# Top-32 attention and two MLPs on one core: the first search step read half from PSUM, head by head

## The chip, the cores and the metric

The kernel runs on one NeuronCore of one Trainium2 chip. The metric is device time in microseconds (us) from one launch. A profiled execution gives a trace with the start and duration of each instruction; its span runs from the first to the last instruction. The engines are TensorE (PE, matmuls into PSUM; PEld is its weight load), VectorE (DVE), ScalarE (ACT), GpSimd (POOL) and SyncE (SP, which only issues transfers here). Each executes its own instructions in a fixed order and waits on semaphores of the others.

## The reference

Attention over 4 batches, 8 heads, 576 positions of width 64, in which each row keeps only its 32 largest scores, then two MLPs on the 2304 resulting rows:

```python
scores = scale * np.matmul(q, k.transpose(0, 1, 3, 2))          # (4, 8, 576, 576)
kth = np.partition(scores, -32, axis=-1)[..., -32:-31]
scores = np.where(scores >= kth, scores, -1e9)
attn = softmax(scores)                                          # rows sum to 1
x = heads_merged(attn @ v)                                      # (2304, 512)
h = x @ w_in                                                    # 512 -> 2048
x = (P(h) / Q(|h|, h*h)) @ w_out                                # P cubic, Q quadratic
h = x @ w2_in
out = (h * np.cos(h)) @ w2_out
```

All in float32.

## The kernel before

Attention is cut into 72 units. A unit is one tile of 128 query rows with one pair of heads: `qk(i)` makes the scores of both heads (`j` is 0 or 1), `topk(i)` finds the 32nd largest of each row, `av(i)` transposes the weights on TensorE and multiplies them with the values. The MLPs follow some units behind in steps `(k, g)`: `in1`, `copy1`, `pol1`, `rec1`, `mid1`, `end1`, `low1`, `out1` for the first (their tiles are `w`, `q`, `r`, `u`, `gg`), `in2` to `out2` for the second.

In `qk`, TensorE writes the scores of one head into `sx`, a PSUM tile of two banks: columns 0 to 287 in one half, 288 to 575 in the other. ScalarE copies them to SBUF, into `sS` (three buffers). There is one `sx`, so the second head's matmuls wait until the first head's copy has been read from it. The spare columns of `sx` serve `av`.

In `topk`, VectorE first takes the larger and the smaller of each score in the left half and its partner in the right half, into the tile `e` (two buffers): two instructions over both heads, 576 columns each. From the larger ones MAX (the eight largest of each row, into `hd`) and MATCH_REPLACE (strike these out) make the first sixteen, then both work over all 576 columns. ScalarE writes the exponentials into `e`, and a SCALAR_TENSOR_TENSOR masks and sums them. A new `e` needs an older one to have been transposed by `av`.

Beside this run 64 conversions (`conv`) of the weights, given in float64, into a high and a low float32 part: SP loads a piece into `raw` (a ring of five buffers, three for the later 32), ScalarE makes two numbers of it, VectorE shifts one (`cb`, a TENSOR_SCALAR), GpSimd adds the two, and the parts are split and stored. GpSimd also does `u` and `q` products, some low parts, and the split of `k` (`store_k`, which follows `qk` in units 1, 3, 5 and 7 and writes `kdr`).

In units 0 to 19 (`U0` is 20) a list scheduler decides the order on each engine, from the order of the code, the data dependencies and a window on how far an engine may run ahead. From unit 20 to 71 the order on the engines is that of the code in `unit`. `free` writes the units before 20: its generator makes `qk(i + 1)`, then steps `topk(i)` and `av(i - 1)` in five pieces, between which `early` puts the MLP steps.

Of the kernel before, what the change touches and what calls it, by code (L numbers as in the profile page):

```python
# [10 lines left out]
F32 = mybir.dt.float32  # L11
# [4 lines left out]
ALU = mybir.AluOpType  # L16
# [3 lines left out]
B, H, S, D = 4, 8, 576, 64  # L20
# [3 lines left out]
P = 128  # L24
# [4 lines left out]
HALF = S // 2  # L29
# [30 lines left out]
OBB, EB, SB = 1, 2, 3  # L60
QRB, QB = 2, 2
S0 = 46
U0, U1 = 20, 72
# [56 lines left out]
def body(tc, out, qt, kt, vt, ident_d, w1_d, w1o_d, a_d, b_d, w2_d, w2o_d):  # L120
    nc = tc.nc
    V, A = InOrder(tc, nc.vector, WIN, C0), InOrder(tc, nc.scalar, WA, PA)
# [3 lines left out]
    with ExitStack() as ctx:  # L126
        def pool(name, bufs=1, **k):
            return ctx.enter_context(tc.tile_pool(name=name, bufs=bufs, **k))
# [4 lines left out]
        att = pool("att", 2)  # L133
# [25 lines left out]
        sx = ps_s.tile([P, 2, 512], F32, name="sx")  # L159
# [17 lines left out]
        def store_k(*a):  # L177
            for _ in split_k(*a):
                pass

        def prep(b, pr):
            x = kv.tile([P, 2, S], F32R, tag="k", bufs=KB, name=f"kraw{b}_{pr}")
            SP.dma_start(out=x[:, 0].bitcast(F32), in_=kt[b, pr])
            return x
# [126 lines left out]
        st, et, sums = {}, {}, {}  # L311
# [3 lines left out]
        def halves(ap):  # L315
            return ap.rearrange("p (a c) -> p a c", a=2)

        def after(mm, bank):
            for x in order[bank]:
                tc.add_manual_dep(mm.ins, x, mybir.DependencyInfo(mybir.DependencyClass.NoSync, mybir.DependencyReason.DATA), reason="bank")  # L320

        def qk(i):
            n, pr = units[i]
            raw, x = qs_.pop(i)
            hi, lo = (x[:, 0], x[:, 1]) if x is not None else (None, None)
            kvs = ins[i]
            m = P // len(kvs)
            st[i] = sb = att.tile([P, 2, S], F32, tag="sS", bufs=SB, name=f"sS{i}")
            for j in range(2):
                rows = slice(j * D, (j + 1) * D)  # L330
                for c, (k, _) in reversed(list(enumerate(kvs))):
                    qs = slice(0, (c + 1) * m)
                    for hf in range(2):
                        o = sx[qs, hf, :HALF]
                        hs = slice(hf * HALF, (hf + 1) * HALF)
                        if n < 2:
                            mm = PE.matmul(o, raw[rows, j, qs], k[rows, 0, hs].bitcast(F32), start=True, stop=True)
                            after(mm, hf)
                        elif i < QH:
                            mm = PE.matmul(o, raw[:, j, qs], k[:, j, hs].bitcast(F32), start=True, stop=True)  # L340
                            after(mm, hf)
                        else:
                            mm = PE.matmul(o, hi[:, j, qs], k[:, j, hs], start=True, stop=False, skip_group_check=True)
                            after(mm, hf)
                            mm = PE.matmul(o, lo[:, j, qs], k[:, j, hs], start=False, stop=True, skip_group_check=True)
                        order[hf] = [mm.ins.name]
                A.activation(halves(sb[:, j]), sx[:, :, :HALF], AF.Copy)
                if j == 0:
                    yield
            if n == 1:  # L350
                store_k(kvs[0][0], 0, pr)

        def topk(i):
            n, pr = units[i]
            sc = st.pop(i)
            tiles = [sc[:, j] for j in range(2)]
            e = att.tile([P, 2, S], F32, tag="e", bufs=EB, name=f"e{i}")
            et[i] = e
            kb, t = n // 2, n % 2
            if i % 8 == 0:  # L360
                sums[kb] = sml.tile([P, 2, H], F32, tag="sum", bufs=2, name=f"sum{kb}")
            sm = sums[kb][:, t]
            hds = sml.tile([P, 2, 32], F32, tag="hd", bufs=2, name=f"hd_{i}")
            hd = [hds[:, j] for j in range(2)]
            nb = sml.tile([P, 2], F32, tag="nb", bufs=2, name=f"nb_{i}")
            big = [e[:, j, :HALF] for j in range(2)]
            both = [e[:, j] for j in range(2)]

            def top(j, x, r):
                V.max(out=hd[j][:, 8 * r:8 * r + 8], in_=x[j])  # L370

            def drop(j, x, r):
                V.match_replace(out=x[j], in_to_replace=hd[j][:, 8 * r:8 * r + 8], in_values=x[j], imm_value=NEG)

            l, r = sc[:, :, :HALF], sc[:, :, HALF:]
            grouped = U0 <= i < U1
            V.tensor_tensor(e[:, :, :HALF], l, r, op=ALU.max)
            if not grouped:
                top(0, big, 0)
                yield  # L380
            V.tensor_tensor(e[:, :, HALF:], l, r, op=ALU.min)
            if not grouped:
                top(1, big, 0)
            yield
            first = ((top, big, 0), (drop, big, 0), (top, big, 1))
            for step in (first[0 if grouped else 1:], ((drop, big, 1), (top, both, 2)), ((drop, both, 2),)):
                for f, *x in step:
                    for j in range(2):
                        f(j, *x)
                yield  # L390
            for j, s in enumerate(tiles):
                top(j, both, 3)
                if j == 0:
                    A.activation(nb, hds[:, :, 0], AF.Copy, scale=-SCALE)
                A.activation(e[:, j], s, AF.Exp, bias=nb[:, j:j + 1], scale=SCALE)
            yield
            for j, s in enumerate(tiles):
                row = sm[:, 2 * pr + j:2 * pr + j + 1]
                V.scalar_tensor_tensor(e[:, j], s, hd[j][:, 31:32], e[:, j], op0=ALU.is_ge, op1=ALU.mult, accum_out=row)
                yield  # L400
# [369 lines left out]
        def free(i, prev):  # L770
            nq = qk(i + 1) if i + 1 < nu else iter(())
            next(nq, None)
            next(nq, None)
            if i + 2 < nu:
                load_k(i + 2)
            t = topk(i) if i < nu else iter([None] * 9)
            fresh = []
            for p in range(5):
                if p == 0:
                    for x, a in held:  # L780
                        store_k(x, *a)
                    held[:] = [(prep(*a), a) for a in preps.get(i, [])]
                    if prev is not None:
                        next(prev)
                    next(t, None)
                    if prev is not None:
                        next(prev)
                    next(t, None)
                    if prev is not None:
                        a = av(i - 1)  # L790
                        next(a)
                        next(a, None)
                        if i % 4 == 0:
                            nrm.append(norm((i - 1) // 8, (i - 1) // 4 % 2))
                            next(nrm[-1])
                            next(nrm[-1])
                            fresh.append(nrm[-1])
                    if 0 < i < nu:
                        load_v(i)
                else:  # L800
                    next(t, None)
                if p == 1 and i < U0:
                    load_q(i + 3)
                if fresh and p == 1:
                    next(fresh.pop())
                if len(nrm) == 2 and p in (1, 4):
                    for x in nrm[:1] if p == 1 else nrm[1:]:
                        next(x)
                        next(x, None)
                    if p == 4:  # L810
                        nrm.clear()
                if i == U0 - 1 and p == 4:
                    for _ in qk(i + 2):
                        pass
                    load_k(i + 3)
                    high_q(i + 3)
                    load_q(i + 4)
                yield t
# [54 lines left out]
        def unit(i, prev):  # L873
            sine = (i - UB - 1) % SINB == SINB - 1
            t = topk(i)
            if i > U0:
                V.ahead = G.last
# [82 lines left out]

        load_k(1)
        load_v(0)
        for _ in qk(0):
            pass
        load_q(2)
        prev = None
        for u in range(UB + NB * NG + 3):
            grouped = U0 <= u < U1
            f = free(u, prev) if not grouped and u <= nu else iter(())
# [55 lines left out]
```

## Time and profile before

| | us |
|---|---|
| median of three runs (1339.94 to 1340.45) | 1340.32 |
| the profiled execution, its own time | 1339.15 |
| its span | 1337.4 |
| TensorE busy in the span | 1233.8 |
| VectorE busy | 1156.0 |
| ScalarE busy | 1093.7 |
| GpSimd busy | 569.6 |

Units 0 to 19 fill the first quarter of the span; in it all engines share the work of attention, of the conversions and, from unit 9, of the first MLP. An engine's busy share over the whole span mixes this part with the later ones, so it has to be read stage by stage. In rows of the trace all instructions stand under one line, L80, where a helper records them; they are told apart by their tiles.

### The profile page before, as it was taken

The page shows a single profiled execution, that of the slowest core. Times are in us where ns is not written, and L with a number is a line of the kernel's source. Part 1 is how long each engine was busy: PE and PEld are TensorE (multiplying, and loading weights), DVE is VectorE, ACT ScalarE, POOL GpSimd, SP SyncE. Part 2 cuts the span into 40 slices and gives each one's busy share as a digit, 9 for nine tenths or more (in the row PEclk, how much of TensorE's full clock was granted, in tenths as well). Part 3 has the DMA queues.
Part 4 walks back from the last instruction along what each step waited for, and adds up shares of the span by engine and source line. Part 5 has one row for each costly group of instructions (what it writes and reads, how often), then busy time and mean ns, then how long its engine had stood idle before and what let it go on. Part 6 is the DMA issues. An engine that isn't in the chain of part 4 may idle for free.

```text
span 1337.4 us, 25132 instructions
## 1 busy us (share of the span) xinstructions
PE 1233.8 (92%) x8992; PEld 1086.7 (81%) x8992; DVE 1156.0 (86%) x2498; ACT 1093.7 (82%) x1871; POOL 569.6 (43%) x469
## 2 busy tenths in 40 slices
PE   6675678888999999999999999999999999999998
PEld 3343455656889999999989899999999999999996
DVE  6999879979799999999999999999999998755633
ACT  7887788886888898888898888888898888877753
POOL 2656444453245555445554444454444444430000
PEclk9676999999999999999999999999999999999999
DMA  8986777884356777667677776666677778877774
GB/s 254 335 278 223 247 239 246 275 311 132 122 190 217 231 245 248 215 218 229 208 234 239 246 230 210 213 217 200 217 234 265 268 283 288 297 235 235 235 258 155
DMA packets 155948, 314.98 MB, mean 236 GB/s; under 512 B 12592, under 2 KB 47536, under 8 KB 155824
## 3 DMA queue, kind: packets, MB, share of 16 engines
q1 hardware_dynamic: 122832, 261.99, 59.3%
q10 hardware_dynamic: 32992, 51.39, 12.0%
q8 instruction: 71, 1.16, 0.4%
q14 instruction: 53, 0.43, 0.1%
HBM read 278.20 MB, written 35.13 MB: 234 GB/s over the span
## 4 chain that ended last, share of the span: by engine, by line
PE 62%; DVE 13%; ACT 12%; DMA 4%; issue 4%; POOL 3%; ACTq 1%; SPq 0%; POOLq 0%; DVEq 0%
PE h L80 24%; PE o L80 12%; PE sx L80 10%; PE y L80 10%; DVE e L80 6%; DVE hd L80 3%; ACT r L80 2%; DVE u L80 2%; DMA raw<-w 1%; ACT sS L80 1%; ACT e L80 1%; ACT cb L80 1%; PE diff L80 1%; DVE cb L80 1%; ACT u L80 1%
## 5 line engine op out<-in xcount | busy, mean ns | idle before, releaser
L80 DVE MAX8 hd<-e 128x8 f32<-128x288 f32 (+1 forms) x576 | 320.9, 595 | 0.0
L80 POOL TENSOR_TENSOR gg<-rr,gg 128x512 fp32r<-128x512 f32 x56 | 72.3, 1292 | 400.8 <-DVE rr L80 185.4
L80 DVE MATCH_REPLACE8 e<-hd,e 128x288 f32<-128x288 f32 (+1 forms) x432 | 230.7, 539 | 0.0
L80 PE MATMUL o<-w2o,gg 128*128 128x512 f32 x864 | 223.6, 398 | 0.0
L80 PE MATMUL y<-gg,w1o 128*128 128x256 f32 x1152 | 216.1, 286 | 7.0 <-ACT gg L80 4.5
L80 PEld LDWEIGHTS y<-gg,w1o 128*128 128x128 f32 x1152 | 182.6, 193 | 12.5 <-ACT gg L80 7.1
L80 PEld LDWEIGHTS o<-w2o,gg 128*128 128x128 f32 x864 | 153.8, 189 | 27.0 <-DVE gg L80 0.3
L80 PE MATMUL h<-xh,w1hi 128*128 128x256 f32 x576 | 171.1, 297 | 4.7 <-ACT xh L80 3.2
L80 PE MATMUL h<-xl,w1hi 128*128 128x256 f32 x576 | 164.2, 285 | 2.5 <-DVE xl L80 2.5
L80 PE MATMUL y<-gg,w1ol 128*128 128x256 f32 x576 | 164.0, 285 | 0.0
L80 PE MATMUL h<-x2l,w2hi 128*128 128x256 f32 x576 | 163.0, 283 | 0.0
L80 PE MATMUL h<-xh,lo 128*128 128x256 f32 x576 | 162.8, 283 | 0.0
L80 PE MATMUL h<-x2h,lo 128*128 128x256 f32 x576 | 162.7, 283 | 0.0
L80 PE MATMUL h<-x2h,w2hi 128*128 128x256 f32 x576 | 162.7, 283 | 0.0
L80 DVE TENSOR_TENSOR e<-sS 128x576 f32<-128x576 f32 x144 | 118.2, 860 | 39.6 <-POOL q L80 27.9
L80 POOL TENSOR_TENSOR cb<-cb,raw 128x512 int32<-128x512 int32 x64 | 88.2, 1383 | 99.7 <-DVE cb L80 75.3
L80 DVE SCALAR_TENSOR_TENSOR e<-sS,hd,e 128x576 f32<-128x576 f32 x144 | 123.0, 882 | 5.9 <-ACT e L80 4.4
L80 PEld LDWEIGHTS h<-xh,w1hi 128*128 128x128 f32 x576 | 109.6, 190 | 17.2 <-issue 5.9
L80 PEld LDWEIGHTS h<-xl,w1hi 128*128 128x128 f32 x576 | 109.9, 191 | 7.7 <-DVE xl L80 4.4
L80 PEld LDWEIGHTS y<-gg,w1ol 128*128 128x128 f32 x576 | 111.4, 193 | 0.7 <-issue 0.4
L80 ACT ACTIVATE e<-sS,nb 128x576 f32<-128x576 f32 x144 | 105.6, 771 | 7.7 <-DVE hd L80 6.0
L80 PEld LDWEIGHTS h<-x2l,w2hi 128*128 128x128 f32 x576 | 110.2, 191 | 0.5 <-issue 0.2
(1026 smaller groups left out, 3272.5 us busy)
## 6 DMA issues: line engine op xcount, KB each, us to landing
w2o<-w2o SPq DMA_DIRECT2D x144, 512.0 KB, 4.2
lo<-w1lo SPq DMA_DIRECT2D x72, 512.0 KB, 3.9
w1ol<-w1ol SPq DMA_DIRECT2D x72, 512.0 KB, 4.8
lo<-w2lo SPq DMA_DIRECT2D x72, 512.0 KB, 4.6
k<-kdr ACTq DMA_DIRECT2D x44, 576.0 KB, 5.6
raw<-w SPq DMA_DIRECT2D x32, 512.0 KB, 5.7
v<-vt ACTq DMA_DIRECT2D x48, 320.0 KB, 4.2
qr<-qt ACTq DMA_DIRECT2D x72, 128.0 KB, 2.7
```

The source lines that it names most:

```text
L80: r = f(*a, **k)
```

## The change

For units 0 to 19 the maxima and minima are taken out of `topk` and made by a new function `pair(i, j)`, for one head at a time. Each instruction covers 288 columns and reads the left half of the scores from `sx` in PSUM and the right half from the copy `sS` in SBUF. `pair(i + 1, 0)` is issued in unit i, behind `av(i - 1)`; then follows the second half of `qk(i + 1)`, that is, head 1's matmuls and copy, and then `pair(i + 1, 1)`. Unit 0's are made before the loop. From unit 20 on nothing is edited.

```diff
+        def pair(i, j):
+            if j == 0:
+                et[i] = att.tile([P, 2, S], F32, tag="e", bufs=EB, name=f"e{i}")
+            for hf, op in enumerate((ALU.max, ALU.min)):
+                V.tensor_tensor(et[i][:, j, hf * HALF:(hf + 1) * HALF], sx[:, 0, :HALF], st[i][:, j, HALF:], op=op)
+
         def topk(i):
             n, pr = units[i]
             sc = st.pop(i)
             tiles = [sc[:, j] for j in range(2)]
-            e = att.tile([P, 2, S], F32, tag="e", bufs=EB, name=f"e{i}")
-            et[i] = e
+            if i >= U0:
+                et[i] = att.tile([P, 2, S], F32, tag="e", bufs=EB, name=f"e{i}")
+            e = et[i]
...
-            V.tensor_tensor(e[:, :, :HALF], l, r, op=ALU.max)
+            if i >= U0:
+                V.tensor_tensor(e[:, :, :HALF], l, r, op=ALU.max)
             if not grouped:
                 top(0, big, 0)
                 yield
-            V.tensor_tensor(e[:, :, HALF:], l, r, op=ALU.min)
+            if i >= U0:
+                V.tensor_tensor(e[:, :, HALF:], l, r, op=ALU.min)
...
         def free(i, prev):
             nq = qk(i + 1) if i + 1 < nu else iter(())
             next(nq, None)
-            next(nq, None)
+            if i + 1 >= U0:
+                next(nq, None)
...
+                    if i + 1 < U0:
+                        pair(i + 1, 0)
+                        next(nq, None)
+                        pair(i + 1, 1)
                     if 0 < i < nu:
                         load_v(i)
...
         load_k(1)
         load_v(0)
-        for _ in qk(0):
-            pass
+        nq = qk(0)
+        for j in range(2):
+            next(nq, None)
+            pair(0, j)
```

Since a scheduler orders units 0 to 19, the built programs differ in more than these lines. The first place is VectorE in unit 7, before; the number behind a tile's letters is the unit (for `cb` the conversion), the one behind the underscore only counts tiles.

```order
L80 TENSOR_TENSOR e7_881<-sS7_741 128x2x288 x2
L80 SCALAR_TENSOR_TENSOR e6_759,sum0_149<-sS6_622,hd_6_760,e6_759 128x576
L80 TENSOR_SCALAR cb0_2_3_855<-cb0_2_3_855 128x512
L80 MAX hd_7_882<-e7_881 128x8 x2
L80 SCALAR_TENSOR_TENSOR e6_759,sum0_149<-sS6_622,hd_6_760,e6_759 128x576
L80 MATCH_REPLACE e7_881<-hd_7_882,e7_881 128x288
L80 TENSOR_SCALAR cb0_3_3_918<-cb0_3_3_918 128x512
L80 MATCH_REPLACE e7_881<-hd_7_882,e7_881 128x288
L80 MAX hd_7_882<-e7_881 128x8 x2
L80 MATCH_REPLACE e7_881<-hd_7_882,e7_881 128x288 x2
```

The two heads take turns there (x2 is one instruction of each head). This is the same place of the changed program:

```order
L80 TENSOR_TENSOR e7_799<-sx_91,sS7_758 128x288 x2
L80 MAX hd_7_897<-e7_799 128x8
L80 MATCH_REPLACE e7_799<-hd_7_897,e7_799 128x288
L80 MAX hd_7_897<-e7_799 128x8
L80 MATCH_REPLACE e7_799<-hd_7_897,e7_799 128x288
L80 MAX hd_7_897<-e7_799 128x8
L80 TENSOR_SCALAR cb1_13_0_973<-cb1_13_0_973 128x512
L80 TENSOR_TENSOR e7_799<-sx_91,sS7_758 128x288 x2
L80 MATCH_REPLACE e7_799<-hd_7_897,e7_799 128x576
L80 TENSOR_SCALAR cb1_12_0_957<-cb1_12_0_957 128x512
```

Head 0's search now runs alone, each instruction behind the one whose result it reads, until head 1's maxima and minima stand in the second couple. The second place is VectorE around the shift of the last conversion, `cb3_15`, before:

```order
L80 TENSOR_SCALAR cb3_14_0_2292<-cb3_14_0_2292 128x512
L80 TENSOR_TENSOR xl1_2491<-xs1_0_1167,xh1_2490 128x512
L80 TENSOR_TENSOR e17_2586<-sS17_2424 128x2x288 x2
L80 MAX hd_17_2587<-e17_2586 128x8 x2
L80 SCALAR_TENSOR_TENSOR e16_2434,sum2_2435<-sS16_2246,hd_16_2436,e16_2434 128x576
L80 SCALAR_TENSOR_TENSOR u0_7_2524<-u0_7_2524,nega_107,w0_7_2521 128x512
L80 SCALAR_TENSOR_TENSOR e16_2434,sum2_2435<-sS16_2246,hd_16_2436,e16_2434 128x576
L80 TENSOR_SCALAR cb3_15_0_2351<-cb3_15_0_2351 128x512
```

And in the changed program:

```order
L80 TENSOR_SCALAR cb3_15_0_2388<-cb3_15_0_2388 128x512
L80 SCALAR_TENSOR_TENSOR e15_2126,sum1_1025<-sS15_2087,hd_15_2286,e15_2126 128x576
L80 TENSOR_SCALAR rs1_1_2501<-sum1_1025 128x8
L80 SCALAR_TENSOR_TENSOR q0_6_2375<-q0_6_2375,r0_6_2376 128x512
L80 SCALAR_TENSOR_TENSOR u0_6_2377<-u0_6_2377,nega_107,r0_6_2376 128x512
L80 RECIPROCAL rs1_1_2501<-rs1_1_2501 128x8
L80 TENSOR_TENSOR e16_2318<-sx_91,sS16_2281 128x288 x2
```

The last shift stood behind the first maxima of unit 17; it now stands ahead of those of unit 16.

## Rows read from the trace of the kernel before

**Rows 1.** The page: busy tenths in 40 slices, and the chain by engine.

```profile
DVE  6999879979799999999999999999999998755633
...
PE 62%; DVE 13%; ACT 12%; DMA 4%; issue 4%; POOL 3%; ACTq 1%; SPq 0%; POOLq 0%; DVEq 0%
```

**Rows 2.** Stretches: length, busy us (x instructions) by engine, granted clock, DMA share.

```profile
12.00:138.00 126.00, 86.00 (x328) 49.75 (x327) 124.74 (x271) 101.29 (x194) 74.92 (x54) 0.78 0.83 273
138.00:296.00 158.00, 124.02 (x733) 92.66 (x733) 130.72 (x271) 130.98 (x250) 74.65 (x54) 0.96 0.81 263
296.00:342.00 46.00, 38.88 (x267) 32.73 (x267) 45.99 (x96) 31.00 (x59) 16.05 (x12) 0.93 0.45 152
342.00:1337.40 995.40, 979.03 (x7659) 908.24 (x7657) 852.99 (x1860) 825.05 (x1362) 403.64 (x343) 1.00 0.70 230
```

**Rows 3.** DVE timeline: the first maxima of units 9, 16 and 20.

```profile
138.06 1.43 DVE L80 TENSOR_TENSOR e<-sS 128x576 f32<-128x576 f32 x2 [0.18 <-PE sx L80]
...
278.54 1.17 DVE L80 TENSOR_TENSOR e<-sS 128x576 f32<-128x576 f32 x1 [0.59 <-PE sx L80]
...
341.95 1.40 DVE L80 TENSOR_TENSOR e<-sS 128x576 f32<-128x576 f32 x2
```

**Rows 4.** Waits of DVE, 12 to 138 us: total, times, longest.

```profile
DVE e L80 <- PE sx L80: 0.6, 2, 0.4
```

**Rows 5.** Waits of DVE, 138 to 296 us.

```profile
DVE cb L80 <- ACT cb L80: 13.2, 6, 6.5
...
DVE e L80 <- PE sx L80: 5.2, 6, 1.8
```

**Rows 6.** Timelines of ACT and DVE at the start of the program.

```profile
6.37 0.65 ACT L80 ACTIVATE sS<-sx 128x576 f32<-128x576 f32 x1 [1.25 <-PE sx L80]
...
10.65 1.43 DVE L80 TENSOR_TENSOR e<-sS 128x576 f32<-128x576 f32 x2 [4.88 <-ACT sS L80]
```

**Rows 7.** DVE timeline near 248 us: start, us, instruction, idle before.

```profile
247.81 0.69 DVE L80 SCALAR_TENSOR_TENSOR q<-q,r 128x512 f32<-128x512 f32 x1 [0.36 <-ACT r L80]
248.42 0.75 DVE L80 SCALAR_TENSOR_TENSOR u<-u,nega,r 128x512 f32<-128x512 f32 x1
249.20 0.69 DVE L80 SCALAR_TENSOR_TENSOR u<-q,u 128x512 f32<-128x512 f32 x1
```

**Rows 8.** DVE by tile, durations min/median/max: `e` to 341 us, others whole span.

```profile
L80 DVE TENSOR_TENSOR e<-sS x40: 731/785/1855, 10.7 to 330.7; 128x576 f32<-128x576 f32 x40
...
L80 DVE TENSOR_TENSOR xl<-xs,xh x18: 668/684/1594, 104.8 to 1171.5; 128x512 fp32r<-128x512 f32 x18
L80 DVE TENSOR_TENSOR xs<-xs,bc x5: 660/670/686, 83.8 to 1169.3; 128x512 f32<-128x512 f32 x5
...
L80 DVE TENSOR_TENSOR x2l<-y,x2h x18: 673/680/692, 323.2 to 1278.9; 128x512 fp32r<-128x512 f32 x18
```

**Rows 9.** DVE groups by shape, 0 to 341 us: busy, mean ns, idle before.

```profile
L80 DVE MAX8 hd<-e 128x8 f32<-128x576 f32 x79 | 56.4, 743 | 0.0
L80 DVE TENSOR_TENSOR e<-sS 128x576 f32<-128x576 f32 x40 | 44.3, 1143 | 11.8 <-PE sx L80 6.6 <-ACT sS L80 5.0
...
L80 DVE MAX8 hd<-e 128x8 f32<-128x288 f32 x80 | 33.0, 443 | 0.0
```

**Rows 10.** Timelines of PE and ACT near 121 us, both heads' matmuls merged.

```profile
120.69 1.13 PE L80 MATMUL sx<-k,qr 128*128 128x288 f32 x4
...
122.37 0.65 ACT L80 ACTIVATE sS<-sx 128x576 f32<-128x576 f32 x1
```

**Rows 11.** One conversion's way: timelines of SP, ACT, DVE and POOL.

```profile
263.50 0.33 SPq L274 DMA_DIRECT2D raw<-w2o  x1
...
269.92 0.66 ACT L80 ACTIVATE raw<-raw 128x512 int32<-128x512 uint32 x1 [2.17 <-DMA raw<-w2o]
...
276.78 0.43 DVE L80 TENSOR_SCALAR cb<-cb 128x512 int32<-128x512 int32 x1 [6.46 <-ACT cb L80]
...
277.28 1.81 POOL L80 TENSOR_TENSOR cb<-cb,raw 128x512 int32<-128x512 int32 x1 [1.91 <-DVE cb L80]
...
279.39 0.38 SPq L274 DMA_DIRECT2D raw<-w2o  x1
```

## Prediction

> **What bounds the kernel now.** I read the digits and the chain of waits of the page first, then busy time by stage, then VectorE's own waits in each stage. Over the whole span TensorE holds 62% of the chain, but that is the long part behind unit 19; the change touches units 0 to 19 only, which end where unit 20's first maximum starts, at 341.95 us [rows 1, 2, 3]. From 342 us on TensorE is busy 979.03 of 995.40 us [rows 2], and nothing there is edited, so I let that stretch keep its length and ask when it starts.
>
> Before it there are three stages. From 12 to 138 us (units 0 to 8) VectorE is busy 124.74 of 126.00 us and its longest wait in all that time sums to 0.6 us [rows 2, 4]: VectorE's instructions, end to end, are the time. From 138 to 296 us (units 9 to 16) it is busy 130.72 of 158.00 us; of the 27 us idle the largest part, 13.2 us, is waiting for ScalarE's part of the weight conversion, and 5.2 us is waiting for TensorE to have read the old `e` [rows 2, 5]. From 296 to 342 us it is full again, 45.99 of 46.00. So what VectorE executes counts nearly one for one in the first and third stage, and in the second as long as the conversions don't wait longer.
>
> **The change, part by part**, against the profiled execution's own 1339.15 us; the median of the three runs is 1.2 us above it.
>
> *The pairs themselves.* 40 maxima and minima of 576 columns from two SBUF tensors become 80 of 288 columns with one operand in PSUM. Undisturbed, two old ones in a row take 1.43 us [rows 6]; neighbours overlap by 0.08 [rows 7], so one takes 0.75 and the next starts 0.68 after it: 40 x 0.68 = 27.2 us. Before has none of the new form. The nearest are those of 512 columns with a PSUM operand, median 0.670 and 0.680 us [rows 8]; a column costs (743 - 443)/288 = 1.04 ns by the two widths of MAX8 [rows 9], so 288 columns take about 0.670 - 224 x 0.00104 = 0.437, and with the same overlap the next starts 0.36 after it: 80 x 0.36 = 28.8. **+1.6 us**. The Trainium skill ("VectorE: DVE Perf Modes", The TRN2 errata) charges a PSUM source 120 fixed cycles against 58 for SBUF, an estimate of 80 x 62 cycles = 5.2 us more at its 0.96 GHz. The rows disagree: with a PSUM operand 0.670, with both in SBUF 0.684, at the same 512 columns [rows 8]; I go by the rows.
>
> *The collisions with GpSimd.* The old ones average 1.143 us, and the longest takes 1.855 [rows 8, 9]; those with a PSUM operand never exceed 0.692 in 23 instances [rows 8]. The excess, 40 x (1.143 - 0.75) = 15.7 us, goes away from these instructions. But GpSimd is still busy 74.92 and 74.65 us in the first two stages [rows 2], and the next instruction with two SBUF inputs can run into the same GpSimd add. In the order of the changed kernel 11 of the 40 new couples are followed at once by a conversion shift, a `u` step or a sum instead of a MAX or MATCH_REPLACE. Bounds: nothing moves on (-15.7) and everything does (0). I take 40% moved, because most neighbours are MAX and MATCH_REPLACE, which show no such excess (443 and 743 mean, with nothing idle before them) [rows 9]: **-9.4 us**.
>
> *The lost interleaving.* Before, the two heads step through the search together, so an instruction rarely reads what the one directly ahead wrote; the built order has 3 such places up to unit 20. Made head by head it has 92, MAX and MATCH_REPLACE of one head in single file, as the order of unit 7 shows. In the trace `u<-u,nega,r` starts 0.08 us before the end of the independent instruction ahead, and `u<-q,u`, which reads it, 0.03 us after its end [rows 7]. 89 x 0.11 = **+9.8 us**. That MAX and MATCH_REPLACE pay the same is not shown; the lower bound is 0.
>
> *The start.* VectorE waits 4.88 us for both copies of unit 0 and starts at 10.65; head 0's copy ended at 6.37 + 0.65 = 7.02 [rows 6]. It can now do head 0's chain (two pairs, three MAX, two narrow MATCH_REPLACE and a wide one, some 3.9 us) while head 1 is made, so nearly all of 3.6 us is used. **-3 us** (bounds 0 and -3.6).
>
> *A round trip in every unit.* The scores of head 1 need the PSUM tile `sx` that VectorE reads for head 0. So between the two couples of a unit lie: two matmuls (half of 1.13 us), ScalarE's copy (0.65), and the queue in front of it (the copy at 122.37 starts 0.55 after the matmuls' end at 121.82) [rows 10]: 1.8 us at that clock, and up to some 3 with the clock granted at 0.78 on average in the first stage [rows 2] and with transposes ahead in TensorE's queue. What covers it is VectorE's work between the couples in the new order: in unit 7 three MAX, two MATCH_REPLACE, four dependent steps and one shift, some 2.7 us; in units 3, 8 and 19 some 2.1. With head 1, `store_k` of units 1, 3, 5 and 7 comes later too (a ScalarE copy, a GpSimd subtraction, four DMAs on SP); its `kdr` is read from unit 8 on, some seven units on, which hides it. While VectorE waits, everything of its queue stands behind, the shifts (`cb`) too, for which GpSimd waits. Bounds 0 and 1 us a unit; I take 0.3 in the 13 units of the full stages (in the middle stage the idle time absorbs it): **+4 us**.
>
> *The order of the conversions.* Nothing in the diff names it, but the scheduler decides it anew. Before unit 16's first maximum stood 59 of the 64 shifts, now all 64; the second place in the section on the change shows the last of them. The ring of three `raw` buffers turns slowly: the load issued at 263.50 is read by ScalarE at 269.92 and leaves GpSimd at 279.09, and 279.39 the next load goes out, 16 us for three, 5.3 us a conversion [rows 11]. If that ring sets the pace of the middle stage, five conversions more before unit 16 keep one unit's work, some 15 us, from running beside them. If VectorE does, it costs nothing. The cb waits are 13.2 of 158 us [rows 5], so I take a fifth: **+3 us**, bounds 0 and +15.
>
> Sum: 1.6 - 9.4 + 9.8 - 3 + 4 + 3 = +6 us. 1339.15 + 6 = 1345 for a profiled execution, and with the 1.2 to the median **1346.3 us**, 0.5% slower. What tells a change here is about 0.2%, 2.7 us.
>
> **Rivals.**
> *Faster: the collisions end and the gaps stay hidden.* All of the 15.7 us is kept and the round trip is covered: 1.6 - 15.7 + 9.8 - 3 = -7.3, a median of 1333. For it: the first stage has no idle time, so every collision there is span. Against: GpSimd's adds follow the shifts and stay where VectorE meets them. A stronger form has the dependent steps free too: -17 us, 1323. The one pair of rows with such a step speaks against it by 0.11 us [rows 7], so that form holds 4 of the 27 in 100 below. The Trainium skill speaks for it ("VectorE: DVE Perf Modes", The DRAIN you can't avoid): a semaphore between VectorE instructions costs nothing extra, since the pipe drains anyhow.
> *Slower by more: the ring decides.* +15 in place of +3: 1358.5. For it: the 6.46 us that VectorE once waited for a shift's input [rows 11], and raw loads that leave right behind GpSimd's adds. Against: 83% busy VectorE in that stage. It decides from the point at which VectorE's waits for `cb` exceed the 13 us of now.
> *It moves nothing.* The couple for unit i+1 still needs the `e` of unit i-1 read by TensorE, and before already waits for that (138.06, 278.54) [rows 3], so "sooner" in the program may not be sooner on the engine, and gains and losses cancel: within 2.7 us of 1340.3.
>
> **Chances.** Forecast (+3 to +13) 0.40; faster rival 0.27; nothing 0.18; ring 0.15. So faster 0.27, same 0.18, slower 0.55. The range for 8 in 10 reaches from 1330 (the faster rival with little moved, without its extreme form) to 1361 (the ring with the round trip a little longer); the forecast's own is 1343 to 1353.
>
> **What would show it.** Right: the new maxima take 0.42 to 0.46 us, none above 0.5; VectorE's busy time before unit 20 falls by less than 8 us; MAX and MATCH_REPLACE of one head start some 0.03 us after the end of the one ahead; waits "`e` for ScalarE's `sS`" of several us in 12 to 138; unit 20's first maximum at about 348. Wrong: a new maximum of over 1 us (PSUM does not spare the collision); sums and shifts with the same means as before (nothing moved on); unit 20 before 340, or TensorE's last stage changing its length of 995 us.

## The result, and the profile after

The changed kernel takes 1350.74 us (median of 6 runs, 1346.83 to 1352.29), the kernel before 1340.13 on the same chip: ratio 1.0067, interval 1.0045 to 1.0089. It is slower, by 9 us going by the ratio and 10.6 by the medians; 1346.3 was predicted, in a range of 1330 to 1361. The profiled execution took 1348.56 us, of which 1346.7 are its span (before: 1339.15 and 1337.4).

The stretches of the changed kernel, cut as in [rows 2] (length, busy time of PE, PEld, DVE, ACT and POOL, granted clock):

```profile
12.00:138.00 126.00, 91.40 (x318) 50.88 (x318) 108.96 (x261) 99.74 (x189) 73.58 (x54) 0.77 0.84 269
138.00:296.00 158.00, 127.71 (x704) 92.15 (x705) 130.52 (x291) 135.02 (x254) 72.52 (x55) 0.90 0.83 271
296.00:342.00 46.00, 34.94 (x239) 30.48 (x238) 42.33 (x95) 26.96 (x50) 10.27 (x8) 0.88 0.31 99
342.00:1346.70 1004.70, 989.68 (x7728) 918.06 (x7727) 860.46 (x1882) 829.49 (x1370) 406.44 (x345) 1.00 0.70 230
...
0.00:355.40 355.40, 271.99 (x1358) 188.53 (x1359) 295.01 (x679) 275.48 (x516) 160.81 (x127) 0.86 0.75 242
```

VectorE, full before in the first stretch (124.74 of 126.00 us), now idles 17 of its 126 us. The last line runs up to unit 20's first maximum. A couple is the maximum and the minimum of one head; the first couples of units 0 and 9, and the first maximum of unit 20, stand on VectorE's timeline at

```profile
7.08 0.82 DVE L80 TENSOR_TENSOR e<-sx,sS 128x288 f32<-128x288 f32 x2 [1.18 <-ACT sS L80]
...
147.00 0.80 DVE L80 TENSOR_TENSOR e<-sx,sS 128x288 f32<-128x288 f32 x2
...
355.53 1.43 DVE L80 TENSOR_TENSOR e<-sS 128x576 f32<-128x576 f32 x2 [4.36 <-PE sx L80]
```

against 10.65, 138.06 and 341.95 before [rows 3, 6]. So the start is 3.6 us sooner, unit 9 is 8.9 us late, unit 20 13.6 us late; 4 us come back behind it (1346.7 - 355.5 = 991.2 us against 995.4). Up to unit 20, VectorE before was busy 302.88 us and idle 39; now it is busy 295.01 and idle 60.5. **The work shrank by 8 us, the idle time grew by 21.5.**

Where the work shrank: VectorE's groups by shape up to unit 20, changed kernel (busy us, mean ns, idle time just before and what ended it):

```profile
L80 DVE SCALAR_TENSOR_TENSOR e<-sS,hd,e 128x576 f32<-128x576 f32 x38 | 39.0, 1025 | 15.3 <-ACT e L80 15.2
L80 DVE TENSOR_SCALAR cb<-cb 128x512 int32<-128x512 int32 x64 | 36.9, 577 | 14.6 <-ACT cb L80 13.6 <-issue 0.7
...
L80 DVE TENSOR_TENSOR e<-sx,sS 128x288 f32<-128x288 f32 x80 | 32.6, 448 | 14.6 <-ACT sS L80 9.9 <-ACT xs L80 4.7
```

and the first two of these groups in the kernel before:

```profile
L80 DVE SCALAR_TENSOR_TENSOR e<-sS,hd,e 128x576 f32<-128x576 f32 x38 | 40.3, 1065 | 1.3 <-ACT e L80 1.3
L80 DVE TENSOR_SCALAR cb<-cb 128x512 int32<-128x512 int32 x64 | 38.2, 600 | 13.2 <-ACT cb L80 13.2
```

The couples fell from 44.3 us [rows 9] to 32.6, and on balance their neighbours took over none of the collisions: the masking steps and the shifts shown here became cheaper, two of the `q` and `u` products dearer (673 to 845 and 738 to 952 ns) and the two others cheaper by more (1141 to 954 and 1017 to 682). The idle time that is new stands mostly in front of the masking step, the SCALAR_TENSOR_TENSOR that needs ScalarE's exponential: 1.3 us before, 15.2 now. In front of the couples it is 14.6 us, where it was 11.8 [rows 9] with the long start in it, and 4.4 stand in front of unit 20's first maximum; the conversions' shifts wait as before.

One unit shows how. VectorE from unit 7's second couple to unit 8's:

```profile
120.74 0.82 DVE L80 TENSOR_TENSOR e<-sx,sS 128x288 f32<-128x288 f32 x2 [0.34 <-ACT sS L80]
...
131.46 0.40 DVE L80 TENSOR_SCALAR cb<-cb 128x512 int32<-128x512 int32 x1
132.38 1.23 DVE L80 SCALAR_TENSOR_TENSOR e<-sS,hd,e 128x576 f32<-128x576 f32 x1 [0.52 <-ACT e L80]
...
133.54 0.81 DVE L80 TENSOR_TENSOR e<-sx,sS 128x288 f32<-128x288 f32 x2
...
137.00 0.82 DVE L80 TENSOR_TENSOR e<-sx,sS 128x288 f32<-128x288 f32 x2 [0.24 <-ACT sS L80]
```

and TensorE and ScalarE in the same stretch:

```profile
123.29 2.05 PE L80 MATMUL diff<-cb,ident 128*128 128x512 f32 x2 [0.84 <-ACT cb L80]
124.34 1.42 PE L80 MATMUL diff<-w1hi,nident 128*128 128x512 f32 x1
125.56 2.12 PE L80 MATMUL sx<-k,qr 128*128 128x288 f32 x4
```

```profile
127.72 0.65 ACT L80 ACTIVATE sS<-sx 128x576 f32<-128x576 f32 x1 [0.61 <-PE sx L80]
...
131.57 0.78 ACT L80 ACTIVATE e<-sS,nb 128x576 f32<-128x576 f32 x1
...
136.32 0.64 ACT L80 ACTIVATE sS<-sx 128x576 f32<-128x576 f32 x1
```

Only at 121.56, with unit 7's second couple, is `sx` free for unit 8. TensorE, in order, has two conversions in front and makes head 0's scores at 125.56; the copy ends at 128.37. The couple stands behind the masking step in VectorE's queue, so that step has nothing in front of it to hide the exponential (131.57 to 132.35) and VectorE waits. The second couple starts at 137.00, 0.04 us after head 1's copy ends at 136.96. Taken unit by unit from such rows, 14 of the 20 second couples start at most 0.1 us after their copy's end; while head 0's copies of units 1 to 19 have lain ready for 7.2 us on average when VectorE comes to them.

### The profile page after: what moved, and what is told of

The parts are those of the page before. It is cut to its first block, busy times and chain, and to the rows that moved or that the text cites. A ratio compares the mean times of both kernels' runs of the same rounds, so it can differ in the third digit from the quotient of the medians.

```text
span 1346.7 us, 25183 instructions
## 1 busy us (share of the span) xinstructions
PE 1248.3 (93%) x8992; PEld 1093.9 (81%) x8992; DVE 1147.2 (85%) x2538; ACT 1096.7 (81%) x1871; POOL 563.2 (42%) x469
## 4 chain that ended last, share of the span: by engine, by line
PE 68%; ACT 11%; DMA 8%; DVE 4%; POOL 4%; issue 3%; ACTq 1%; SPq 0%; POOLq 0%; DVEq 0%
PE h L80 27%; PE o L80 13%; PE sx L80 12%; PE y L80 11%; DMA raw<-w 2%; DVE e L80 2%; POOL cb L80 2%; PE diff L80 2%; ACT r L80 1%; ACT cb L80 1%; ACT e L80 1%; DMA raw<-w2o 1%; DMA raw<-w1o 1%; ACT sS L80 1%; ACT u L80 1%
## 5 line engine op out<-in xcount | busy, mean ns | idle before, releaser
L80 DVE MAX8 hd<-e 128x8 f32<-128x576 f32 (+1 forms) x576 | 325.2, 598 | 1.5
L80 POOL TENSOR_TENSOR cb<-cb,raw 128x512 int32<-128x512 int32 x64 | 85.8, 1343 | 103.3 <-DVE cb L80 89.4
L80 PEld LDWEIGHTS h<-xh,lo 128*128 128x128 f32 x576 | 111.3, 193 | 0.1
L80 PEld LDWEIGHTS h<-x2h,w2hi 128*128 128x128 f32 x576 | 110.2, 191 | 0.4
```

The source lines that it names most:

```text
L80: r = f(*a, **k)
```

## The experiments

Each ran against the kernel before on the same chip. "Unit 20" is the start of its first maximum in the run's profiled execution; busy and idle are VectorE's up to there. That one execution can lie some us beside the median, which decides (in e7 it is 5 us below, in e8 5 above). "Steps" counts, up to unit 20 in the built order, the VectorE instructions that read what the one directly ahead wrote. The first two lines repeat the runs above. The kernel before took 1341.2 us beside e1 to e4, 1342.7 beside e5 to e8, 1341.2 beside e9 to e11 and 1343.5 beside e12, so versions of different groups are best compared by their ratios.

| version | median us | ratio to before | unit 20 | busy | idle | steps |
|---|---|---|---|---|---|---|
| before | 1340.13 | 1 | 341.9 | 302.9 | 39.0 | 3 |
| changed | 1350.74 | 1.0067 [1.0045, 1.0089] | 355.5 | 295.0 | 60.5 | 92 |
| e1_sbuf | 1344.16 | 1.0020 [1.0004, 1.0037] | 347.3 | 311.8 | 35.5 | 25 |
| e2_split | 1341.76 | 0.9997 [0.9983, 1.0010] | 342.1 | 307.4 | 34.7 | 9 |
| e3_both | 1341.29 | 1.0002 [0.9985, 1.0019] | 350.4 | 287.0 | 63.4 | 4 |
| e4_bothcover | 1346.34 | 1.0047 [1.0026, 1.0068] | 354.6 | 286.4 | 68.2 | 3 |
| e5_first | 1339.68 | 0.9978 [0.9963, 0.9992] | 339.9 | 299.8 | 40.1 | 15 |
| e6_twin | 1325.80 | 0.9874 [0.9853, 0.9895] | 332.3 | 292.8 | 39.5 | 33 |
| e7_to11 | 1346.56 | 1.0033 [1.0013, 1.0053] | 342.0 | 293.7 | 48.3 | 51 |
| e8_twin11 | 1327.41 | 0.9890 [0.9870, 0.9910] | 333.7 | 293.6 | 40.1 | 9 |
| e9_beforetwin | 1333.86 | 0.9935 [0.9915, 0.9955] | 336.0 | 297.1 | 38.9 | 1 |
| e10_sbuftwin | 1333.95 | 0.9942 [0.9921, 0.9962] | 330.6 | 307.5 | 23.1 | 23 |
| e11_twinfile | 1340.35 | 0.9991 [0.9974, 1.0008] | 346.0 | 298.2 | 47.8 | 74 |
| e12_sbufhold | 1353.17 | 1.0085 [1.0062, 1.0108] | 353.8 | 317.5 | 36.3 | 71 |

My first theory was the order of the heads (dependent steps and bare masking steps). Its rival, called A from e3 on, is the round trip through the PSUM tile; in e1, A is the move to one unit sooner. B is the ring of the conversions.

**Both halves from SBUF, same place (e1).**

```
-    V.tensor_tensor(et[i][:, j, hf * HALF:(hf + 1) * HALF], sx[:, 0, :HALF], st[i][:, j, HALF:], op=op)
+    V.tensor_tensor(et[i][:, j, hf * HALF:(hf + 1) * HALF], st[i][:, j, :HALF], st[i][:, j, HALF:], op=op)
```

> The couples stay per head and one unit sooner, but both operands come from the copy in SBUF, so the PSUM tile of the scores is free again as soon as ScalarE has copied it; the built order then has 25 dependent steps up to unit 20 (92 in the changed kernel, 3 before). Theory (the collisions really ended; the loss is head-by-head order, about 11 us of dependent steps and about 20 us of idle VectorE because scores are no longer made ahead): the couples rise from 0.448 us to 0.6 or more (some +12 us), dependent steps cost 2.7 us, and the waits of the masking step for ScalarE's exponential fall from 15 to under 5 us; together 1340 to 1347. Rival A (making them a unit sooner is itself what costs, by the scheduler's order): the idle time stays at about 60 us and the collisions come on top: 1358 to 1365. Rival B (the raw ring of the conversions): it has 57 shifts before unit 16 and so the time is under 1340.

Its couples, up to unit 20:

```profile
L80 DVE TENSOR_TENSOR e<-sS 128x288 f32<-128x288 f32 x80 | 54.1, 716 | 18.2 <-ACT sS L80 14.3 <-PE sx L80 3.8
```

716 ns against 448: the collisions are back, and yet the kernel is faster than the changed one, since the idle time falls from 60.5 to 35.5 us. So being a unit sooner costs little by itself (e1 is 0.2% above the kernel before, and below rival A's 1358 to 1365); reading PSUM, or what goes with it, costs more.

**Before, cut into heads (e2).** In `topk` of units 0 to 19 the two instructions of 576 columns became four of 288, head by head, from SBUF.

> The kernel before with its two instructions of 576 columns in units 0 to 19 cut into four of 288, head by head, in the old place and from SBUF: the cut alone. 9 dependent steps against 3. Theory: 40 more starts (80 x 0.36 against 40 x 0.68 is +1.6) and 6 x 0.12 = 0.7 for steps, so 1340 to 1344; the couples keep their collisions (mean of one over 0.55 us). Rival (the cut into heads is what costs, wherever it stands): 1348 or more.

No change from before, as expected: the cut alone is not it.

**The interleaving restored, PSUM kept (e3), and the masking step covered as well (e4).**

```
         def pair(i, j):
...
+            made[i, j] = r.ins.name
...
             def top(j, x, r):
-                V.max(out=hd[j][:, 8 * r:8 * r + 8], in_=x[j])
+                m = V.max(out=hd[j][:, 8 * r:8 * r + 8], in_=x[j])
+                if (i, 1) in made and r == 0 and j == 0:
+                    tc.add_manual_dep(m.ins, made[i, 1], ORDER, reason="both")
...
+                if (i + 1, 0) in made:
+                    tc.add_manual_dep(m.ins, made[i + 1, 0], ORDER, reason="cover")
```

These are e4's lines; `r` is the last instruction of the couple. e3 has the same without the last two, which stand at the masking step.

> The changed kernel with the first maximum of a unit held behind the last minimum of its head 1, so that the search interleaves the heads again (4 dependent steps), with the PSUM operand kept. Theory (order): dependent steps give back 10.5 us, the masking step's waits for the exponential fall from 15 to under 6 us, and the wait for head 1's copy grows from 10 to some 15 to 20, as it stands bare now: 1334 to 1343. Rival A (the round trip through the PSUM tile is the loss, as predicted): it is paid in full, 20 units x 1 to 1.5 us more, 1355 to 1370. Rival B (conversions' ring): as the changed kernel, 1349 to 1353, since 63 shifts still stand before unit 16.

> As the one before, and the masking step of a unit is held behind head 0's couple of the next unit, which gives the exponential something to hide behind (3 dependent steps). Theory (order): the masking step waits under 3 us in all, the wait for head 1's copy is 10 to 20: 1332 to 1342, not above the one before by more than 3. Rival A (round trip): 1355 to 1370. Rival B (ring): 1349 to 1353.

In e3 VectorE's groups of masking steps and couples up to unit 20 are

```profile
L80 DVE SCALAR_TENSOR_TENSOR e<-sS,hd,e 128x576 f32<-128x576 f32 x38 | 36.9, 984 | 10.4 <-ACT e L80 10.3
L80 DVE TENSOR_TENSOR e<-sx,sS 128x288 f32<-128x288 f32 x80 | 32.7, 450 | 19.6 <-ACT sS L80 16.8 <-ACT xs L80 2.7
```

Time and steps came out as my theory had it: 8 us less work for 88 steps fewer, and a kernel as fast as the one before. But its idle time did not: 63.4 us, and 68.2 with the masking steps covered. Part of the wait moved from the exponential to the scores. e4, at 1346.3, missed its range of 1332 to 1342; both runs lie outside rival A's 1355 to 1370 and rival B's 1349 to 1353. So the order costs some 9 us of the time, but it is not the cause of the idle time.

**Unit 0 alone (e5).** The conditions `i < U0` of the change became `i == 0`.

> The change in unit 0 alone; units 1 to 19 as before. Both theories: VectorE starts 3.5 us sooner, at 7.1 us. If that start is kept, the time is 3 us under the kernel before (1337); if the first stage then waits elsewhere, no change (1340). The built order has 15 dependent steps up to unit 20 where before has 3, which takes up to 1.4 us of it back.

3 us faster (1 to 5 by its interval): the start is kept.

**A second PSUM tile for head 1 (e6), and the change in units 0 to 10 alone without it (e7) and with it (e8).** The two banks are those that `y` takes from unit 11 on; both heads' scores are then made ahead. The matmuls, the copy and `pair` take `sbank(i, j)[0]` in place of `sx`.

```
+TW = 11
...
+        sy = ps_y.tile([P, 2, 512], F32, tag="y", name="sy")
+
+        def sbank(i, j):
+            return (sy, 2) if j and i < TW else (sx, 0)
...
-            if i + 1 >= U0:
+            if i + 1 >= U0 or i + 1 < TW:
                 next(nq, None)
```

> The changed kernel with a second PSUM tile for head 1's scores in units 0 to 10 (two banks that the block behind attention uses only from unit 11 on), so that TensorE makes both heads' scores ahead though VectorE reads PSUM; units 11 to 19 as in the changed kernel. The scheduler then leaves 33 dependent steps where the changed kernel has 92. Theory H (the loss is the PSUM tile being held until VectorE has read it: TensorE and ScalarE fall into step with VectorE): unit 9 starts at 128 to 138 instead of 147, ScalarE's wait for scores and VectorE's for the exponential in the first stage shrink to under 4 us together, and the time falls to 1336 to 1344. Theory O (head-by-head order): unit 9 gains only what the fewer dependent steps give, about 6 us for the whole, starts at 142 or later, and the waits for the exponential stay near 7 us in the first stage; 1343 to 1348.

> The change in units 0 to 10 alone, one PSUM tile; units 11 to 19 as before. Theory H: the loss up to unit 9 stays (unit 9 starts at 144 to 150), and units 11 to 19 lose nothing; 1344 to 1350. Theory O: in the same way 1344 to 1350; this run is the partner of the next one.

> As the run before, with the second PSUM tile for head 1's scores: the only difference is whether the tile is held. 9 dependent steps. Theory H: unit 9 starts at 126 to 136, 10 us or more sooner than in the run before, and the time is the lowest of all, 1328 to 1338. Theory O: the difference to the run before is that of 42 dependent steps, 5 us, and unit 9 starts at about 142; 1340 to 1345. If unit 9 is early and the time is not, something else than VectorE's work sets when the long last stage ends.

In e6 the copies of one unit's heads and VectorE's couples on them:

```profile
87.52 0.68 ACT L81 ACTIVATE sS<-sy 128x576 f32<-128x576 f32 x1
93.02 0.65 ACT L81 ACTIVATE sS<-sx 128x576 f32<-128x576 f32 x1
```

```profile
95.30 0.81 DVE L81 TENSOR_TENSOR e<-sy,sS 128x288 f32<-128x288 f32 x2
...
103.52 0.81 DVE L81 TENSOR_TENSOR e<-sx,sS 128x288 f32<-128x288 f32 x2
...
125.17 0.81 DVE L81 TENSOR_TENSOR e<-sy,sS 128x288 f32<-128x288 f32 x2
```

Head 1's scores lie ready 7.1 us and head 0's 9.9 us before VectorE comes, and unit 9 starts at 125.17 instead of 147.00. All that VectorE waits for from 12 to 126 us is

```profile
DVE e L81 <- PE sx L81: 1.5, 1, 1.5
DVE e L81 <- ACT sS L81: 1.0, 1, 1.0
DVE cb L81 <- issue: 0.5, 1, 0.5
```

where the changed kernel waits 15.8 us from 12 to 138:

```profile
DVE e L80 <- ACT e L80: 6.7, 8, 1.6
DVE cb L80 <- ACT cb L80: 5.2, 4, 1.8
DVE e L80 <- ACT xs L80: 2.1, 1, 2.1
DVE e L80 <- ACT sS L80: 1.1, 4, 0.3
DVE cb L80 <- issue: 0.7, 1, 0.7
```

e6 is faster than both kernels, by 1.3% against before, and below the range of 1336 to 1344 of the theory that it was to test. e8 against e7, which differ in the second tile alone (and in the order that the scheduler makes of it), gives 19 us. And e8 equals e6: whether units 11 to 19 have the change makes no difference that can be measured.

**Is it the tile itself (e9, e10)?** e9 is before and e10 is e1, each with `sy` in units 0 to 10.

> The kernel before, with the second PSUM tile for head 1's scores in units 0 to 10 and nothing else: a control on whether the tile by itself is what gained. Theory H (the tile only takes back what the PSUM operand costs in holding; before, ScalarE's copy frees the tile at once and VectorE is full): within 4 us of the kernel before, with the collisions as they are, couples of 576 columns at a mean above 1 us. Rival (a second tile speeds any order of these units): 1330 or less.

> The couples per head, a unit sooner and from the SBUF copy alone, with the second PSUM tile in units 0 to 10: the same control for the changed order. Theory H: as the SBUF version without the tile, 1340 to 1346, with the couples' sum still near 57 us. Rival (the second tile and the early scores gain, not the PSUM operand): 1325 to 1333.

Both expectations missed on the same side: the second tile is worth 7 to 9 us to before and 10 us to e1. So of the 25 us between the changed kernel and e6, 7 to 10 go to any order of these units and, by difference, 15 to 18 to the PSUM operand. In e9 the idle time stays at 38.9 us; the couples are cheaper, not rid of collisions, but met by fewer:

```profile
L81 DVE TENSOR_TENSOR e<-sS 128x576 f32<-128x576 f32 x41 | 39.0, 981 | 7.9 <-ACT sS L81 5.3 <-PE sx L81 2.6
```

against 1143 ns [rows 9]. (The row counts one instruction of unit 20; the mean of the other 40 is 986. Of these 13 take over 0.8 us; before, 20.) Read across by the ratios, the PSUM operand costs 6 us with one tile (1.0067 against 1.0020) and gains 9 with two (0.9874 against 0.9942).

**More dependent steps (e11).** e6, and in units 0 to 10 head 1's first MATCH_REPLACE held behind head 0's last.

> The version with the second tile, and in units 0 to 10 head 1's search held behind head 0's last wide MATCH_REPLACE: 74 dependent steps up to unit 20 instead of 33, nothing else changed in the work. If a dependent step costs the 0.12 us that the gaps in the trace show, and VectorE is the bound there, the time is 4 to 6 us over the version without it, 1329 to 1333. If dependent steps are hidden or free: the same, 1325 to 1327.

41 steps more and 5.4 us more work (298.2 against 292.8): 0.13 us each. But the kernel, expected at 1329 to 1333, lost 14.5 us, of which 8.3 show as idle time up to unit 20 (47.8 against 39.5): single file costs beyond its steps.

**The hold without the PSUM operand (e12).** e1, with TensorE's first score matmul of a head made to wait for the couple of the head before (`r` is the last instruction of that couple).

```
+                        if hf == 0 and i < U0:
+                            for x in holds:
+                                tc.add_manual_dep(mm.ins, x, WAIT, reason="hold")
...
+            holds[:] = [r.ins.name]
```

> The version that reads both halves from SBUF with one PSUM tile (1344.2), and in it a wait put in by hand: TensorE may make the next head's scores only when VectorE has made the couple of the head before, as the PSUM operand forces in the changed kernel. Nothing reads PSUM that did not, and the collisions are as without the wait. Theory H (holding the tile costs, about 15 us by the runs with a second tile): 1352 to 1364, with VectorE's idle time up to unit 20 above 50 us where it was 35.5. Rival (it is the read of PSUM itself, not the holding): 1342 to 1347.

1353.2, 9 us above e1: holding the tile costs though nothing reads PSUM. Its form was not the expected one: 36.3 us idle, not over 50, and 317.5 us busy:

```profile
0.00:353.80 353.80, 258.66 (x1327) 179.86 (x1328) 317.49 (x680) 270.79 (x511) 164.65 (x126) 0.87 0.73 242
```

The scheduler answered the hold with 46 more dependent steps (46 x 0.12 = 5.5 us). So the hold's cost in time is shown without the PSUM operand; that it takes the form of idle time is not. What the four versions share that hold the tile in all 20 units (the changed one, e3, e4 and e12) is the time at which unit 20 starts, 350.4 to 355.5 us, while VectorE's work up to there differs by 31 us (286.4 to 317.5).

## Why the prediction was right, and where it was wrong

The direction was right, and the time within the forecast's own 1343 to 1353, but two terms were mis-sized in opposite directions. Two of its signs came out the other way: unit 20, named at about 348, starts at 355.5, and the last stretch changed its length.

*The pairs* (+1.6): right. The new instruction takes 0.448 us, 0.437 was forecast; none lasts longer than 0.46. Two in a row take 0.82, and what follows starts 0.37 us for each after the first, 80 x 0.365 = 29.2 against the 28.8 forecast.

*The collisions* (-9.4): too small. I let 40% move to neighbours. On balance none did: the shifts went from 600 to 577 ns, the masking steps from 1065 to 1025, which the text named as a sign that nothing moves on, and the `q` and `u` products from 35.7 to 34.2 us together, two of them up and two down. From start to next start, 40 x (1.143 - 0.07) = 42.9 us became 29.2: -13.7, where 1.6 - 15.7 = -14.1 would be all of it. (The 443 and 743 ns given there for MAX and MATCH_REPLACE are both MAX's [rows 9].)

*The lost interleaving* (+9.8): right. In the changed kernel the search of unit 7 begins

```profile
117.23 0.44 DVE L80 MAX8 hd<-e 128x8 f32<-128x288 f32 x1
117.71 0.09 DVE L80 MATCH_VALUE_LOAD e<-hd,e 128x8 f32 x1
117.78 0.44 DVE L80 MATCH_REPLACE8 e<-hd,e 128x288 f32<-128x288 f32 x1
118.26 0.46 DVE L80 MAX8 hd<-e 128x8 f32<-128x288 f32 x1
```

The MAX at 118.26 starts 0.04 us after the end of the MATCH_REPLACE that it reads; an independent one starts 0.08 before the end (the shift at 131.46 starts 0.08 before the MAX ahead of it ends, 130.79 + 0.75). e3 takes 88 of the 92 steps away and 8.0 us of work with them (0.09 each), e11 adds 41 and 5.4 us (0.13 each). The Trainium skill ("VectorE: DVE Perf Modes", The DRAIN you can't avoid) says, of a chain of copies, that the semaphores between them cost nothing extra. These MAX and MATCH_REPLACE chains differ from it by 0.09 to 0.13 us a step.

*The start* (-3): right; VectorE starts 3.6 us sooner, and e5 keeps 3 us.

*The order of the conversions* (+3): no sign of it. Waits for `cb` sum to 13.6 us where they were 13.2, and from unit 9 to 17 both kernels take 158 us. e3 has 63 of the 64 shifts ahead of unit 16 and is as fast as the kernel before; e1 has 57 and is no faster. No run changed that order alone.

*The round trip in every unit* (+4): **this step failed.** It asked for one wait, between the two couples of a unit, found it covered by VectorE's search but for 0.3 us in 13 units, and set an upper bound of 1 us a unit.

The trip itself was read too short. The four rows at 120.69 [rows 10] are one head's matmuls, not both heads', as four rows to each copy show in the kernel before, up to 342 us:

```profile
L80 PE MATMUL sx<-k,qr x104: 403/406/846, 116.9 to 337.5; 128*128 128x288 f32 x104
...
L80 PE MATMUL sx<-kraw,qr x64: 402/644/846, 4.0 to 101.7; 64*128 64x288 f32 x64
L80 ACT ACTIVATE sS<-sx x42: 623/643/680, 6.4 to 338.0; 128x576 f32<-128x576 f32 x42
```

So the trip starts with all of the 1.13 us and not half of it, at a granted clock of 1.0 (2.4 GHz), and with 2.12 us at 125.56 in the changed kernel, where 0.50 (1.2 GHz) was granted. With the 0.55 and 0.65 us behind, that is 2.3 or 3.3 us, where the forecast had 1.8 and up to some 3. Measured from the end of head 0's couple to the end of head 1's copy it is 2.3 to 5.7 us, 3.9 on average, and VectorE idles 8.7 us directly ahead of the second couples, where 4 were forecast.

That is the smaller part. The idle time grew by 21.5 us though the start gave 3.6 back: 25 us, or 1.25 a unit, above that bound. What the step left out is that the tile is also what lets scores be made ahead. Held until VectorE reads it, it binds TensorE's and ScalarE's queues, full of conversions, to VectorE's place in the program twice a unit. The loss then shows wherever VectorE runs out of cover: mostly at the masking step, 14 us more than before (the forecast had several us of waits for `sS` in 12 to 138; they sum to 1.1, those for the exponential to 6.7), and at the couples, which also wait 4.7 us for `xs`, the copy of the attention output from other columns of `sx`. The second tile takes the idle time back to 39.5 us with every PSUM operand kept (e6), and the hold alone costs 9 us where nothing reads PSUM, though there as longer work (e12).

At the sum: the terms of work were forecast at +2.0 and came to -8 (counting each instruction from the end of the one ahead, couples -13, search +8.6, neighbours -3.7), those of idle time at +4 and came to +21.5, of which 3 are the gaps in front of dependent steps. Of the 13.5 that this makes, 4 were given back behind unit 20, whose stretch I took as fixed. The forecast of 6 was near the 9.3 of the span partly by luck, because these errors cancel.

**The last stretch.** From unit 20's first maximum to the end it lasts 988 to 1002 us over these versions. TensorE, busy nearly all of it [rows 2], makes there what it has not made before. It has made 1372 of its 8992 matmuls by then in e3, and 1282 in e10 (the first count in each row),

```profile
0.00:350.40 350.40, 258.87 (x1372) 182.92 (x1373) 287.02 (x681) 275.04 (x519) 162.19 (x127) 0.89 0.75 247
...
0.00:330.60 330.60, 247.31 (x1282) 172.62 (x1283) 307.51 (x674) 266.18 (x507) 164.56 (x125) 0.88 0.78 257
```

and the stretch then takes 988.4 and 1001.6 us. Over the fourteen versions it is 0.11 us shorter for each matmul made sooner (correlation 0.97); no run changed that count alone. So a unit 20 that starts late is paid back as far as TensorE has worked ahead.

**What stays open.** Why a hold shows as idle time in one version and as single file in another: the scheduler makes a new order each time, and no run held the order still. And what beyond the steps the single file of e11 costs.

## What to carry to other kernels

An operand read from PSUM in place of the copy that another engine has made is cheap by itself and spares VectorE the collisions, but it makes the slowest reader the owner of the tile. Before pricing the instruction, ask who could write that tile ahead of time until now; if the answer is an engine with an in-order queue of other work, find a second tile first (here two banks that stand empty until a later stage), and take the two together. When the wait moves each time that one order is mended (e3, e4), the order is not the cause of the wait; look for the resource that all the orders share.

## What the runs showed of the hardware

VectorE's maxima and minima of 288 columns take 0.448 us on average with one operand in PSUM whatever GpSimd does, and 0.716 with both in SBUF (e1). In the changed kernel 42 of the 80 run beside a GpSimd instruction, and all 80 stay under 0.46. In the kernel before, 20 of the 40 of 576 columns take over 0.8 us, and each of these runs beside one; of the 20 others one does. The Trainium skill ("SBUF — State Buffer", Who interferes with whom) has the two engines lock a port pair against each other; by that section a VectorE instruction with two SBUF inputs contends with a GpSimd instruction that reads SBUF. These rows agree: with one of the two in PSUM none was held up. How often they collide depends on timing: the same 40 instructions take 1143 ns on average before and 986 in e9, which changes only where TensorE writes, and with it the order that the scheduler makes.
